# The gate products of a fused attention, expert and gate kernel as seven block products

## The chip, the cores and the metric

The kernel runs on one core of a Trainium2 chip. The metric is device time in microseconds (us) of one execution. TensorE (PE in the profile) multiplies, VectorE (DVE), ScalarE (ACT) and GpSimd (POOL) do the elementwise work, and SyncE (SP) issues the transfers.

## The reference

Three networks in a row. Attention with global and local keys gives `x` (1536 tokens x 512); a mixture of four experts turns it into a new `x` of the same shape; the last part, which the change touches, is:

```python
def _moe2_ref(x, w1, w2, w3, w_out):     # x 1536x512, w1 and w2 512x1024, w3 1024x1024, w_out 1024x512
    a = x @ w1
    b = x @ w2
    h = a * b @ w3
    return (h @ w_out).astype(np.float32)
```

The kernel takes the four weights of this part as float64 words and converts them to float32 on the chip while the experts run.

## The kernel before

Every product is made of blocks of 128x128 (stationary) by 128x512 (moving) and in three matmuls: an operand `x` is kept as two tiles of type fp32r, `hi` (its rounding) and `lo` (what the rounding left), and `three` (lines 52 to 56) adds hi*hi, hi*lo and lo*hi in one PSUM bank. `split` (lines 46 to 49) makes the two tiles: ACT casts, DVE (or POOL, if asked) subtracts.

The 1536 tokens are three chunks of 512. All engines run their instructions in the order in which the code issues them (`manual_schedule`), so that order is the schedule. After the attention and the experts, `experts_and_gate` does two things:

- the w34 stage (`for j in range(FC)`, 8 steps of 24 matmuls): w3 times w_out, once, with one split of the result per step and, behind it on ACT and DVE, the split (`land`) of the weight block that was loaded the step before. The weight block for step j + 4 is loaded in step j into the place `slots[4 + j % 4]` that step j used.
- the gate stage: for each chunk c and each of 8 blocks f of 128 hidden columns, `gate` makes a = x @ w1 and b = x @ w2 (2 x 12 matmuls of 512 columns), multiplies them, splits the product; `final`, one step later, adds its 12 matmuls into four PSUM banks. After the last f of a chunk four copies (`o`) and four transfers write its 512 rows of the output.

The PSUM pool `ps_z` has four banks for products, `ps_a` the four banks of `final`. `x_hi[c]`, `x_lo[c]` hold x split, `acc[c]` holds it whole. `slots` are eight pairs of tiles 128x1024 for split weights, and `wr` are two tiles for weights as they come from memory.

Of the kernel before, what the change touches and what calls it, by code (L numbers as in the profile page):

```python
# [8 lines left out]
F32 = mybir.dt.float32  # L9
F32R = mybir.dt.float32r  # L10
# [3 lines left out]
ALU = mybir.AluOpType  # L14
# [4 lines left out]
P = 128  # L19
# [506 lines left out]
def experts_and_gate(tc, g, x_hi, x_lo, slots, experts, first_time):  # L526

    nc = tc.nc
    name = "" if first_time else "g"
    with ExitStack() as ctx:  # L530
        big = ctx.enter_context(tc.tile_pool(name=name + "big", bufs=1))
        pool = ctx.enter_context(tc.tile_pool(name=name + "mp", bufs=2))
        ps_z = ctx.enter_context(tc.tile_pool(name=name + "ps_z", bufs=4, space=PSUM))
        ps_a = ctx.enter_context(tc.tile_pool(name=name + "ps_a", bufs=1, space=PSUM))
        acc = [big.tile([P, KC, CW], F32, name=f"acc{c}") for c in range(NCH)]
# [66 lines left out]
        for n, w in enumerate(work):  # L602
            if n >= done:
# [3 lines left out]
                elif coming:  # L607
                    s = coming[-1][0] + 1
# [12 lines left out]
            if n > 4 and n % FC not in (LAG - 1, LAG):  # L621
# [34 lines left out]
        pend = {}  # L656
        work2 = [(c, f) for c in range(NCH) for f in list(range(4, FC)) + list(range(4))]
        first, last = 4, 3

        def gate(c, f):  # L660
            hi, lo = slots[f]
            za = ps_z.tile([P, CW], F32, name="z")
            zb = ps_z.tile([P, CW], F32, name="z")
# [12 lines left out]
        def final(c, f):
            hh, hl = pend.pop((c, f))
            if f == first:
                g.acc_ps = [ps_a.tile([P, DM], F32, name=f"o{d}") for d in range(TPC)]
            for j in range(TPC):  # L680
                js = slice(j * P, (j + 1) * P)
                three(nc, g.acc_ps[j], hh[:, js], hl[:, js], w34h[:, f], w34l[:, f], f == first, f == last)
            if f == last:
                for j in range(TPC):
                    o = wpool.tile([P, DM], F32, name="o", bufs=4)
                    if j % 2:
                        nc.scalar.copy(o, g.acc_ps[j])
                    else:
                        nc.vector.tensor_copy(o, g.acc_ps[j])
                    t0 = c * CW + j * P  # L690
                    nc.sync.dma_start(g.out[t0 : t0 + P, :], o)
# [12 lines left out]
def tile_attention_experts_gate(
# [117 lines left out]
```

## Time and profile before

| | us |
|---|---|
| time, median of 3 runs | 854.98 (854.77 to 855.07) |
| the profiled execution's own time | 855.01 |
| its span, first to last instruction | 853.2 |
| PE busy in the span | 843.0 (99%), 4102 matmul records |
| DVE, ACT, POOL busy | 363.4 (43%), 242.2 (28%), 228.8 (27%) |
| mean granted clock | 0.998 |

The profile is of one execution. PE is the matmul engine and PEld its weight load. Matmuls are pipelined: a record's length is longer than the distance to the next one's start, and the ends are modelled, so the pace is read from starts. A timeline row reads: start, duration (both us), engine, line, operation, output <- inputs, shape, count, and in brackets the idle time before it and what ended it.

### The profile page before, as it was taken

What the parts mean: (1) busy time and instruction counts of PE and PEld (TensorE: products, weight loads), DVE (VectorE), ACT (ScalarE), POOL (GpSimd) and SP (SyncE); (2) the same over time, 40 slices, a digit from 0 to 9 for tenths busy, and PEclk for the clock granted to TensorE, in tenths of its full rate; (3) what the DMA queues carried; (4) which work ended last, traced back from release to release, by engine and by line L of the source; (5) the groups of instructions that cost most, each with busy time, mean ns of one, the idle gap of its engine ahead of it and who ended that gap; (6) DMA issues with size and microseconds to landing.
All of it is one profiled execution on the core that took longest, in us unless ns stands there. A gap on an engine that the chain in (4) does not pass through costs nothing.

```text
span 853.2 us, 10750 instructions
## 1 busy us (share of the span) xinstructions
PE 843.0 (99%) x4102; PEld 687.2 (81%) x4102; DVE 363.4 (43%) x745; ACT 242.2 (28%) x517; POOL 228.8 (27%) x246
## 2 busy tenths in 40 slices
PE   8999999999999999999999999999999999999996
PEld 4777888888888888888888888888888888888885
DVE  7998354547654547654223412123343412112111
ACT  6997221223221223221112201113233311111111
POOL 3687012514344445554120202121300000000000
PEclk9999999999999999999999999999999999999999
DMA  7761242548352537451203300002332201000001
GB/s 215 220 212 62 76 136 73 154 133 248 110 161 75 160 126 242 139 148 62 87 1 111 121 3 0 1 1 87 99 124 77 72 0 50 1 1 31 20 1 53
DMA packets 34287, 78.68 MB, mean 92 GB/s; under 512 B 3576, under 2 KB 10024, under 8 KB 34228
## 3 DMA queue, kind: packets, MB, share of 16 engines
q1 hardware_dynamic: 34228, 77.92, 29.2%
q8 instruction: 34, 0.56, 0.3%
q14 instruction: 25, 0.20, 0.1%
HBM read 64.25 MB, written 13.66 MB: 91 GB/s over the span
## 4 chain that ended last, share of the span: by engine, by line
PE 90%; POOL 3%; ACT 3%; DVE 1%; issue 1%; DMA 0%; SPq 0%; POOLq 0%; ACTq 0%; DVEq 0%
PE z L56 17%; PE z L55 17%; PE z L54 17%; PE o L56 13%; PE o L55 13%; PE o L54 13%; ACT pt L268 2%; POOL pt L307 2%; POOL sl L49 1%; ACT ptT L293 0%; DMA words<-in_n_local_dram 0%; PE sp L54 0%; DVE t L261 0%; PE sp L55 0%; PE sp L56 0%
## 5 line engine op out<-in xcount | busy, mean ns | idle before, releaser
L56 PE MATMUL z<-xh,sl 128*128 128x512 f32 x564 | 219.4, 389 | 0.0
L54 PE MATMUL z<-xh,sh 128*128 128x512 f32 x564 | 219.4, 389 | 0.0
L55 PE MATMUL z<-xl,sh 128*128 128x512 f32 x564 | 219.4, 389 | 0.0
L519 DVE SCALAR_TENSOR_TENSOR hl<-z,hh 128x512 fp32r<-128x512 f32 x93 | 64.2, 692 | 271.9 <-ACT hh L518 271.8
L518 ACT ACTIVATE hh<-z 128x512 fp32r<-128x512 f32 x93 | 55.4, 598 | 369.3 <-PE z L56 369.3
L54 PE MATMUL o<-hh,sh 128*128 128x512 f32 x384 | 149.5, 389 | 0.0
L55 PE MATMUL o<-hl,sh 128*128 128x512 f32 x384 | 149.4, 389 | 0.0
L56 PE MATMUL o<-hh,sl 128*128 128x512 f32 x384 | 149.4, 389 | 0.0
L56 PEld LDWEIGHTS z<-xh,sl 128*128 128x128 f32 x564 | 105.9, 188 | 22.3
L55 PEld LDWEIGHTS z<-xl,sh 128*128 128x128 f32 x564 | 105.9, 188 | 22.0
L54 PEld LDWEIGHTS z<-xh,sh 128*128 128x128 f32 x564 | 105.9, 188 | 21.8
L497 POOL TENSOR_TENSOR cr<-cr,cb 128x512 f32<-128x512 f32 x40 | 51.6, 1289 | 159.8 <-issue 153.5
L573 POOL TENSOR_TENSOR acc<-acc,t 128x512 f32<-128x512 f32 x36 | 47.6, 1343 | 161.3 <-DVE t L572 94.9
L54 PEld LDWEIGHTS o<-hh,sh 128*128 128x128 f32 x384 | 72.1, 188 | 15.1
L56 PEld LDWEIGHTS o<-hh,sl 128*128 128x128 f32 x384 | 72.1, 188 | 15.0
L55 PEld LDWEIGHTS o<-hl,sh 128*128 128x128 f32 x384 | 72.1, 188 | 14.8
L670 DVE TENSOR_TENSOR t<-z,t 128x512 f32<-128x512 f32 x24 | 16.6, 692 | 130.6 <-PE z L56 130.6
L49 DVE TENSOR_TENSOR sl<-wr,sh 128x1024 fp32r<-128x1024 f32 x49 | 60.4, 1235 | 26.1 <-ACT sh L48 26.0
L482 POOL TENSOR_SCALAR ca<-ca 128x512 f32<-128x512 f32 x40 | 59.6, 1489 | 37.0 <-DMA raw<-in_w_out_dram 37.0
L48 ACT CAST sh<-wr 128x1024 fp32r<-128x1024 f32 (+1 forms) x61 | 56.0, 920 | 5.4 <-DMA wr<-w3t_d 4.4
L268 ACT ACTIVATE pt<-t,negmax 128x256 f32<-128x256 f32 (+1 forms) x96 | 45.9, 479 | 9.0 <-DVE negmax L261 7.7
L307 POOL TENSOR_TENSOR pt<-pt,r 128x256 f32<-128x256 f32 (+1 forms) x72 | 40.8, 594 | 15.3 <-DVE r L236 12.6
(104 smaller groups left out, 846.8 us busy)
## 6 DMA issues: line engine op xcount, KB each, us to landing
wr<-in_w_moe_dram SPq DMA_DIRECT2D x32, 512.0 KB, 4.6
raw<-in_w3t_dram SPq DMA_DIRECT2D x16, 512.0 KB, 4.6
raw<-in_w_ab_dram SPq DMA_DIRECT2D x16, 512.0 KB, 4.2
raw<-in_w_out_dram SPq DMA_DIRECT2D x8, 512.0 KB, 5.7
w3t_d<-cr SPq DMA_DIRECT2D x16, 256.0 KB, 2.3
wab_d<-cr SPq DMA_DIRECT2D x16, 256.0 KB, 2.3
wr<-w3t_d SPq DMA_DIRECT2D x8, 512.0 KB, 3.4
wr<-wab_d SPq DMA_DIRECT2D x8, 512.0 KB, 3.2
```

Source lines behind the costliest of these rows:

```text
L48: nc.scalar.copy(hi, src)
L49: (lo_engine or nc.vector).tensor_tensor(lo, src, hi.bitcast(F32), op=ALU.subtract)
L54: nc.tensor.matmul(out, wh, xh, start=start, stop=False)
L55: nc.tensor.matmul(out, wh, xl, start=False, stop=False)
L56: nc.tensor.matmul(out, wl, xh, start=False, stop=stop)
L268: nc.scalar.activation(pt[:, hh, 0:w], t[:, 0:w], AF.Exp, bias=g.negmax[:, u * H + h : u * H + h + 1], scale=-1.0, accum_out=sums[:, h : h ...
L307: nc.gpsimd.tensor_tensor(pt[:, hh, 0:w], pt[:, hh, 0:w], r[:, hh : hh + 1].to_broadcast([P, w]), op=ALU.mult)
L482: nc.gpsimd.tensor_scalar(a, a, 2.0**-15, None, op0=ALU.max)
L497: nc.gpsimd.tensor_tensor(rest, rest, top.bitcast(F32), op=ALU.add)
L518: nc.scalar.activation(hh, z, AF.Relu)
L519: nc.vector.scalar_tensor_tensor(hl, z, 0.0, hh.bitcast(F32), op0=ALU.max, op1=ALU.subtract)
L573: nc.gpsimd.tensor_tensor(acc[c][:, d], acc[c][:, d], t, op=ALU.add)
```

## The change

For each f, the two products a and b of the gate form one block product: the rows are (w1 block, w2 block), the inner dimension is two halves of 256, and the columns are two groups of tokens. Done straight, it takes 8 products of blocks; the new class `Gate` does it in 7 by Strassen's scheme in Winograd's form, with sums of weight blocks (s1 to s4), sums of x blocks (t1 to t4), and sums of the products. In pair 0 the two groups are the halves of chunk 0 (256 tokens each), in pair 1 they are chunks 1 and 2 (512 each). The output of the last chunk is computed at the very end, from gated tiles that are kept aside in memory that has come free.

- In the w34 stage, weight blocks 4 to 7 of w3 go through two places (`slots[4]`, `slots[5]`) in place of four; block 6 is loaded in step 4 and split in step 5, block 7 in steps 5 and 6.
- Sums of x are made in DVE in steps 3 and 6, their splits in step 5; the first f's weights are prepared in steps 4 and 7.
- Weights are fetched and split for each f of each pair: 16 loads in place of 8, with the low parts made on POOL.
- The tile `o` for the output has 2 buffers in place of 4.

The core of the diff (index arithmetic of `Gate` left out):

```diff
-            hi, lo = slots[4 + j % 4]
+            hi, lo = slots[4 + (j if j < 4 else j % 2)]
...
             split(nc, w34h[:, j], w34l[:, j], z)
             land()
-            load_slot(4 + j % 4, g.w3t_f32[j + 4] if j < 4 else g.wab_f32[j])
+            if j in (0, 1, 4, 5):
+                load_slot(4 + j % 4 % 2, g.w3t_f32[{0: 4, 1: 5, 4: 6, 5: 7}[j]])
+            if j == 3:
+                gate.sums_of_x(0)
+                gate.fetch()
+            if j == 4:
+                gate.split_w(True)
+                gate.sums_of_w()
+            if j == 5:
+                for n in range(4):
+                    gate.split_x(0, n)
+            if j == 6:
+                gate.sums_of_x(1)
+            if j == 7:
+                gate.rest_of_acc()
+                gate.fetch()
+                gate.split_s(slots[4])
...
-            for z, o0 in ((za, 0), (zb, CW)):
-                for k in range(KC):
-                    ks = slice(o0 + k * P, o0 + (k + 1) * P)
-                    three(nc, z, hi[:, ks], lo[:, ks], x_hi[c][:, k], x_lo[c][:, k], k == 0, k == KC - 1)
...
+            o = wpool.tile([P, DM], F32, name="o", bufs=2)
...
+        for pair in range(2):
+            ps = [ps_a.tile([P, DM], F32, name=f"o{d}") for d in range(TPC)]
+            before = None
+            for f in range(FC + 1):
+                between = [()] * 4
+                if before:
+                    between = [(lambda j=j, h=before, f=f - 1: final(ps, h, f, (j,))) for j in range(TPC)]
+                if f < FC:
+                    before = gate.run(pair, f, between)
+                else:
+                    for j, issue in enumerate(between):
+                        issue()
+                        put(ps[j], pair, j)
+        for j in range(TPC):
+            z = {j: ps_z.tile([P, CW], F32, name="z")}
+            for f in range(FC):
+                final(z, gate.waiting[f], f, (j,))
+            put(z[j], NCH - 1, j)
...
+    def sums_of_w(self, part=None):
...
+        todo = ((s1, a21, a22, ALU.add), (s2, s1, a11, ALU.subtract), (s3, a11, a21, ALU.subtract),
+                (s4, a12, s2, ALU.subtract))
+        for out, a, b, op in todo if part is None else todo[part : part + 1]:
+            self.nc.vector.tensor_tensor(out, a, b, op=op)
+
+    def split_s(self, place=None):
+        y = place or self.places.pop(0)[1]
+        for c in (slice(0, 512), slice(512, F)):
+            split(self.nc, y[0][:, c], y[1][:, c], self.sums[:, c], self.nc.gpsimd)
...
+    def run(self, pair, f, between):
+        w = CW if pair else CW // 2
...
+        nc.scalar.copy(s1, product("a11", "b11"))
+        add(s6, s1, product("s2", "t2"))
+        if more:
+            self.split_w()
+        issue(0)
+        add(c11, s1, product("a12", "b21"))
+        part(0)
+        part(1)
+        add(u3, s6, product("s3", "t3"))
+        part(2)
+        part(3)
+        if more:
+            self.split_s()
+        issue(1)
+        z = product("s1", "t1")
+        add(c22, u3, z)
...
+        add(h2, s6, z)
+        issue(2)
+        z = product("a22", "t4")
...
+        add(h1, u3, z)
+        nc.vector.tensor_tensor(h1, h1, c11, op=ALU.mult)
+        split(nc, *halves[0], h1)
+        issue(3)
+        add(h2, h2, product("s4", "b22"))
+        nc.vector.tensor_tensor(h2, h2, c22, op=ALU.mult)
+        split(nc, *halves[1], h2)
+        if not pair and f in (2, 4):
+            self.split_x(1, 1 if f == 2 else 3)
+        if not pair and f == FC - 1:
+            self.split_x(1, 0)
+            self.split_x(1, 2)
+            self.make_waiting()
+        return hh, hl
```

`product` takes a bank `z` of `ps_z`, and issues `three` twice (the two parts of the inner half): 6 matmuls of w columns. `add` is a DVE addition of 128 x w; `issue(n)` issues the three matmuls of `final` for output rows n of the f before; `part(n)` makes one sum of the next f's weights; `split_w` splits the next f's plain weight blocks (768 columns).

On ACT, the end of the w34 stage stood like this before (`w34h<-z` splits the result of steps 5, 6 and 7, `sh4` to `sh6` are places of split weights, of which those written here are first read in the gate stage):

```order
L48 CAST w34h_5264<-z_5419 128x512 [waits PE_49]
L48 CAST sh4_1556<-wr_5417 128x1024 [waits DMAHW4_49,DVE_49]
L48 CAST w34h_5264<-z_5450 128x512 [waits PE_49]
L48 CAST sh5_1558<-wr_5448 128x1024 [waits DMAHW5_49,DVE_49]
L48 CAST w34h_5264<-z_5481 128x512 [waits PE_49]
```

and stands like this now (`z_5430`, `z_5469`, `z_5502` are the results of steps 5, 6 and 7; step 6 reads `sh4`, step 7 reads `sh5`):

```order
L48 CAST w34h_5264<-z_5430 128x512 [waits PE_49]
L48 CAST sh4_1556<-wr_5415 128x1024 [waits DMAHW3_49,DVE_49]
L48 CAST sh6_1560<-acc0_1576 128x512 [waits DVE_49] x2
L48 CAST sl6_1561<-acc0_1576 128x512 [waits DVE_49]
L48 CAST sl6_1561<-acc0_1576 128x512
L48 CAST w34h_5264<-z_5469 128x512 [waits PE_49]
L48 CAST sh5_1558<-wr_5459 128x1024 [waits DMAHW4_49,Activation_49]
L48 CAST w34h_5264<-z_5502 128x512 [waits PE_49]
L48 CAST sh4_1556<-sums_5425 128x512 [waits DVE_49]
L48 CAST sh4_1556<-sums_5425 128x512
```

The cast of a weight place stands behind the result of the step that comes right ahead of the step that reads it; the sums of the first f's weights stand behind the result of step 7.

On PE, the w34 stage passed to the gate stage like this before (the last matmul of step 7, then the first product of `gate`):

```order
L56 MATMUL z_5481<-sh3_83,sl7_1563 128x512
L54 MATMUL z_5514<-xh0_71,sh4_1556 128x512 [waits Activation_49]
L55 MATMUL z_5514<-xl0_74,sh4_1556 128x512 [waits Pool_49]
L56 MATMUL z_5514<-xh0_71,sl4_1557 128x512 [waits DVE_49]
L54 MATMUL z_5514<-xh0_71,sh4_1556 128x512
```

and does like this now (the last matmul of step 7, the product a11 b11, and the first three matmuls of s2 t2, whose stationary operands `sh4`, `sl4` hold the sums):

```order
L56 MATMUL z_5502<-sh3_83,sl5_1559 128x512
L54 MATMUL z_5543<-xh0_71,hh_5417 128x256
L55 MATMUL z_5543<-xl0_74,hh_5417 128x256 [waits Pool_49]
L56 MATMUL z_5543<-xh0_71,hl_5418 128x256 [waits Pool_49]
L54 MATMUL z_5543<-xh0_71,hh_5417 128x256
L55 MATMUL z_5543<-xl0_74,hh_5417 128x256
L56 MATMUL z_5543<-xh0_71,hl_5418 128x256
L54 MATMUL z_5551<-sl6_1561,sh4_1556 128x256 [waits Activation_49]
L55 MATMUL z_5551<-sl7_1563,sh4_1556 128x256
L56 MATMUL z_5551<-sl6_1561,sl4_1557 128x256 [waits Pool_49]
```

The matmuls now have 256 columns, and the second product waits for ACT's and POOL's split of sums.

On ACT, the passage from chunk 0 to the next one was this before (`o` is an output copy, `z_5939` the first product of chunk 1):

```order
L48 CAST hh_5911<-t_5908 128x512 [waits DVE_49]
L687 COPY o_5930<-o1_5587 128x512 [waits PE_49]
L687 COPY o_5936<-o3_5589 128x512 [waits PE_49]
L669 COPY t_5965<-z_5939 128x512 [waits PE_49,Activation_49]
L48 CAST hh_5968<-t_5965 128x512 [waits DVE_49]
```

and is this now, from pair 0 to pair 1 (`sh0`, `sh1` take the last two split sums of x, `prob_6328` is s1 of pair 1's first f):

```order
L48 CAST hh_6273<-t_6261 128x256 [waits DVE_49]
L48 CAST sh0_77<-acc1_1577 128x1024 [waits PE_49,Pool_49]
L48 CAST sh1_79<-acc1_1577 128x1024 [waits PE_49,Pool_49]
L683 COPY o_6309<-o1_5539 128x512 [waits PE_49]
L683 COPY o_6321<-o3_5541 128x512 [waits DMAHW0_49,PE_49,Activation_49]
L835 COPY prob_6328<-z_6329 128x512 [waits PE_49]
```

The second output copy now waits for a transfer (DMAHW0, the output of the first copy), and the copy that frees the first product's bank stands behind it.

## Rows read from the trace of the kernel before

**Rows 1.** The page: busy time, and the chain that ended last

```profile
PE 843.0 (99%) x4102; PEld 687.2 (81%) x4102; DVE 363.4 (43%) x745; ACT 242.2 (28%) x517; POOL 228.8 (27%) x246
PE 90%; POOL 3%; ACT 3%; DVE 1%; issue 1%; DMA 0%; SPq 0%; POOLq 0%; ACTq 0%; DVEq 0%
```

**Rows 2.** Timeline: first matmul of the w34 stage, last matmul of the kernel

```profile
606.92 0.39 PE L54 MATMUL z<-sh,sh 128*128 128x512 f32 x1
...
846.06 0.39 PE L56 MATMUL o<-w34h,hl 128*128 128x512 f32 x1
```

**Rows 3.** Timeline of weight loads, one burst of the attention scores

```profile
29.64 0.30 PEld L250 LDWEIGHTS sp<-keys,qr 64*128 64x128 f32 x4 [0.17 <-issue]
```

**Rows 4.** Tile sp: durations (ns, least/median/most) of loads and matmuls

```profile
L250 PEld LDWEIGHTS sp<-keys,qr x18: 182/186/187, 29.6 to 36.0; 64*128 64x128 f32 x18
L250 PE MATMUL sp<-keys,qr x18: 376/376/480, 29.6 to 36.0; 64*128 64x256 f32 x18
```

**Rows 5.** Timeline around the end of one step of the w34 stage

```profile
639.34 0.39 PE L56 MATMUL z<-sh,sl 128*128 128x512 f32 x1
639.34 0.19 PEld L54 LDWEIGHTS z<-sh,sh 128*128 128x128 f32 x1
639.56 0.39 PE L54 MATMUL z<-sh,sh 128*128 128x512 f32 x1
639.76 0.59 ACT L48 CAST w34h<-z 128x512 fp32r<-128x512 f32 x1 [3.90 <-PE z L56]
...
640.25 1.06 ACT L48 CAST sh<-wr 128x1024 fp32r<-128x1024 f32 x1
640.38 0.69 DVE L49 TENSOR_TENSOR w34l<-z,w34h 128x512 fp32r<-128x512 f32 x1 [3.27 <-ACT w34h L48]
641.34 1.23 DVE L49 TENSOR_TENSOR sl<-wr,sh 128x1024 fp32r<-128x1024 f32 x1 [0.26 <-ACT sh L48]
```

**Rows 6.** Groups by shape: busy us, mean ns, idle before

```profile
L400 DVE TENSOR_TENSOR xl<-op,xh 128x256 fp32r<-128x256 f32 x24 | 9.9, 413 | 0.6 <-ACT xh L394 0.4
L49 DVE TENSOR_TENSOR hl<-t,hh 128x512 fp32r<-128x512 f32 x24 | 16.6, 693 | 16.5 <-ACT hh L48 16.5
L311 DVE TENSOR_SCALAR pt<-pt,r 128x256 f32<-128x256 f32 x20 | 12.4, 618 | 0.1
L394 ACT CAST xh<-op 128x256 fp32r<-128x256 f32 x24 | 8.8, 367 | 0.6 <-PE op L326 0.6
L48 ACT CAST hh<-t 128x512 fp32r<-128x512 f32 x24 | 14.9, 621 | 69.2 <-DVE t L670 69.2
L48 ACT CAST sh<-wr 128x256 fp32r<-128x256 f32 x12 | 4.9, 405 | 0.0
L576 POOL TENSOR_TENSOR xl<-acc,xh 128x512 fp32r<-128x512 f32 x12 | 15.5, 1290 | 8.8 <-ACT xh L575 8.8
L49 POOL TENSOR_TENSOR sl<-wr,sh 128x256 fp32r<-128x256 f32 x12 | 8.7, 728 | 0.6 <-ACT sh L48 0.3
```

**Rows 7.** The page, DMA issues: KB each, median us to landing

```profile
wr<-wab_d SPq DMA_DIRECT2D x8, 512.0 KB, 3.2
out_dram<-o SPq DMA_DIRECT2D x12, 256.0 KB, 2.6
```

**Rows 8.** Tile out_dram: the twelve output transfers

```profile
DMA to landing us min/median/max: 2.1/2.6/4.6
```

**Rows 9.** Timeline: the last output copy

```profile
846.48 0.59 ACT L687 COPY o<-o 128x512 f32<-128x512 f32 x1 [0.77 <-PE o L56]
```

**Rows 10.** Windows: busy us by engine (instructions), granted clock, DMA share, GB/s

```profile
16.00:100.00 84.00, 82.83 (x735) 62.89 (x734) 67.78 (x254) 66.71 (x226) 50.45 (x96) 1.00 0.47 146
848.00:849.00 1.00, 0.00 (x0) 0.00 (x0) 0.00 (x0) 0.00 (x0) 0.00 (x0) 1.00 1.10 385
850.00:851.00 1.00, 0.00 (x0) 0.00 (x0) 0.00 (x0) 0.00 (x0) 0.00 (x0) 0.50 0.08 16
```

More of the change, by code (lines that the diff above doesn't have):

```diff
@@ L676, in final @@
[L676 to L691, printed above, removed]
@@ new lines, in experts_and_gate, with final @@
+            if j == 5:
[7 more added lines that the diff above has]
+                gate.split_s(slots[4])
+        def final(ps, hid, f, js, f0=0, f1=FC - 1):
+            hh, hl = hid
+            for j in js:
+                ts = slice(j * P, (j + 1) * P)
+                three(nc, ps[j], hh[:, ts], hl[:, ts], w34h[:, f], w34l[:, f], f == f0, f == f1)
@@ new lines, in put @@
+        def put(ps, c, j):
+            o = wpool.tile([P, DM], F32, name="o", bufs=2)
+            if j % 2:
+                nc.scalar.copy(o, ps)
+            else:
+                nc.vector.tensor_copy(o, ps)
+            t0 = c * CW + j * P
+            nc.sync.dma_start(g.out[t0 : t0 + P, :], o)
+        for pair in range(2):
[7 more added lines that the diff above has]
+                    before = gate.run(pair, f, between)
+                else:
+                    for j, issue in enumerate(between):
+                        issue()
+                        put(ps[j], pair, j)
@@ new lines, in experts_and_gate, with __init__, rest_of_acc, make_waiting @@
+        for j in range(TPC):
[3 more added lines that the diff above has]
+            put(z[j], NCH - 1, j)
+class Gate:
+    def __init__(self, tc, g, big, pool, ps_z, wpool, hidden, x_hi, x_lo, acc, slots):
+        self.nc, self.g, self.big, self.pool, self.ps_z, self.wpool = tc.nc, g, big, pool, ps_z, wpool
+        self.hidden = hidden
+        self.x_hi, self.x_lo, self.acc, self.slots = x_hi, x_lo, acc, slots
+        self.order = [(pair, f) for pair in range(2) for f in range(FC)]
+        self.fetched, self.sums, self.made = [], None, []
+        halves = lambda t: [t[i][:, h * CW : (h + 1) * CW] for i in range(2) for h in range(2)]
+        self.parts = [
+            list(zip(halves(slots[6]), halves(slots[7]))), [slots[0], slots[2], slots[1], slots[3]],
+        ]
+        self.places = [(slots[0], slots[1]), (slots[4], slots[5])] * 4 + [(slots[6], slots[7]), (slots[4], slots[5])] * 4
+    def rest_of_acc(self):
+        t = self.big.tile([P, KC, CW], F32, name="acc0")
+        self.tmp = [t[:, i] for i in range(KC)]
+    def make_waiting(self):
+        self.waiting = [(self.x_hi[0][:, i], self.x_lo[0][:, i]) for i in range(KC)]
+        h, l = (self.big.tile([P, KC, CW], F32R, name=f"acc{i}") for i in (1, 2))
+        self.waiting += [(h[:, i], l[:, i]) for i in range(KC)]
+    def block(self, of, pair, k, n):
+        ks = slice(2 * k, 2 * k + 2)
+        if pair:
+            return of[1 + n][:, ks]
+        return of[0][:, ks, n * (CW // 2) : (n + 1) * (CW // 2)]
+    def sums_of_x(self, pair):
+        sub = lambda out, a, b: self.nc.vector.tensor_tensor(out, a, b, op=ALU.subtract)
+        b11, b12, b21, b22 = (self.block(self.acc, pair, k, n) for k in range(2) for n in range(2))
+        sub(b11, b12, b11)
+        sub(b12, b22, b12)
+        sub(b22, b22, b11)
+        sub(b21, b21, b22)
+    def parts_of(self, pair, n):
+        return [t.rearrange("p (k t) -> p k t", k=2) for t in self.parts[pair][n]]
+    def split_x(self, pair, n):
+        split(self.nc, *self.parts_of(pair, n), self.block(self.acc, pair, n // 2, n % 2))
+    def x_operand(self, pair, what):
+        if what[0] == "b":
+            k, n = int(what[1]) - 1, int(what[2]) - 1
+            return self.block(self.x_hi, pair, k, n), self.block(self.x_lo, pair, k, n)
+        return self.parts_of(pair, "1342".index(what[1]))
+    def fetch(self):
+        if self.order:
+            pair, f = self.order.pop(0)
+            raw = self.pool.tile([P, F], F32, name="wr")
+            self.nc.sync.dma_start(raw, self.g.wab_f32[f])
+            self.fetched.append(raw)
+    def split_w(self, first=False):
+        raw = self.fetched[0]
+        if first:
+            a, b = ([self.hidden.tile([P, CW], F32R, name=n) for n in ("hh", "hl")] for _ in range(2))
+        else:
+            a, b = [t[:, 0:512] for t in self.places[0][0]], [t[:, 512:768] for t in self.places[0][0]]
+        b = [t[:, 0:256] for t in b]
+        split(self.nc, *a, raw[:, 0:512], self.nc.gpsimd)
+        split(self.nc, *b, raw[:, 768:], self.nc.gpsimd)
+        part = lambda of, i: [t[:, i * 256 : (i + 1) * 256] for t in of]
+        self.blocks = dict(a11=part(a, 0), a12=part(a, 1), a22=b)
+    def sums_of_w(self, part=None):
+        if part in (None, 0):
+            self.sums = self.wpool.tile([P, F], F32, name="sums")
+        raw = self.fetched[0]
+        a11, a12, a21, a22 = (raw[:, i * 256 : (i + 1) * 256] for i in range(4))
+        s1, s2, s3, s4 = (self.sums[:, i * 256 : (i + 1) * 256] for i in range(4))
+        todo = ((s1, a21, a22, ALU.add), (s2, s1, a11, ALU.subtract), (s3, a11, a21, ALU.subtract),
[6 more added lines that the diff above has]
+            split(self.nc, y[0][:, c], y[1][:, c], self.sums[:, c], self.nc.gpsimd)
+        for i in range(4):
+            self.blocks[f"s{i + 1}"] = [t[:, i * 256 : (i + 1) * 256] for t in y]
+        self.made.append(self.blocks)
+        self.fetched.pop(0)
+        self.fetch()
+    def run(self, pair, f, between):
+        nc = self.nc
+        w = CW if pair else CW // 2
+        blocks = self.made.pop(0)
+        def product(a, b):
+            z = self.ps_z.tile([P, CW], F32, name="z")[:, 0:w]
+            h, l = blocks[a]
+            xh, xl = self.x_operand(pair, b)
+            for k in range(2):
+                ks = slice(k * P, (k + 1) * P)
+                three(nc, z, h[:, ks], l[:, ks], xh[:, k], xl[:, k], k == 0, k == 1)
+            return z
+        def issue(n):
+            if between[n]:
+                between[n]()
+        more = bool(self.fetched)
+        add = lambda out, a, b: nc.vector.tensor_tensor(out, a, b, op=ALU.add)
+        part = (lambda n: self.sums_of_w(n)) if more else (lambda n: None)
+        s1 = self.pool.tile([P, CW], F32, name="prob")[:, 0:w]
+        s6, u3, c22, c11 = (t[:, 0:w] for t in self.tmp)
+        nc.scalar.copy(s1, product("a11", "b11"))
[14 more added lines that the diff above has]
+        add(c22, u3, z)
+        h2 = self.pool.tile([P, CW], F32, name="t", bufs=3)[:, 0:w]
+        add(h2, s6, z)
+        issue(2)
+        z = product("a22", "t4")
+        if pair:
+            hh = self.hidden.tile([P, CW], F32R, name="hh")
+            hl = self.hidden.tile([P, CW], F32R, name="hl")
+            halves = [(hh, hl), self.waiting[f]]
+        else:
+            hh = self.hidden.tile([P, CW], F32R, name="hh")
+            hl = self.hidden.tile([P, CW], F32R, name="hl")
+            halves = [(hh[:, 0:w], hl[:, 0:w]), (hh[:, w:], hl[:, w:])]
+        h1 = self.pool.tile([P, CW], F32, name="t", bufs=3)[:, 0:w]
+        add(h1, u3, z)
[12 more added lines that the diff above has]
+        return hh, hl
```

23 lines of the change are left out of this document (1 added, 22 removed).

## The prediction

> **What bounds the kernel now.** I read the page's busy times and chain first [rows 1]: PE is busy for 99% of the span and 90% of the chain is PE. The question is then whether PE waits or runs at its pace, and the starts answer that: from the first matmul of the w34 stage to the last of the kernel there are 8 x 24 + 864 = 1056 matmuls, started from 606.92 to 846.06 [rows 2], so 239.14 / 1055 = 0.2267 us each, which is also the distance of two neighbours (639.34 and 639.56 [rows 5]). There is no gap: this stretch is matmul count times 0.2267, and a stall anywhere in it adds in full. What follows the last matmul is a copy that starts 0.42 later and takes 0.59 [rows 9], and an output transfer.
>
> **What is removed.** The gate stage has 3 chunks x 8 f x (24 + 12) = 864 matmuls of 512 columns, 195.9 us. After the change pair 1 has 8 x 7 x 6 = 336 matmuls of 512 columns (384 before for the same two chunks), `final` keeps its 288: 624 x 0.2267 = 141.5 us. Pair 0 has 8 x 7 x 6 = 336 matmuls of 256 columns where 192 of 512 were. So the change saves 54.4 us less 336 times p, the pace at 256 columns, which no row shows for this type.
>
> **The pace p.** 0.2267 at 512 columns is 512 / 2.4 GHz = 0.213 plus 0.013. If the 0.013 belongs to each matmul, p is 0.107 + 0.013 = 0.120. It can't be below what the load of 128 weight columns takes. A load's record is 0.19 long and begins with its predecessor's matmul [rows 5], yet records overlap: the four loads of one burst [rows 3], two for each half of the array, end 0.30 after the first one's start, so the second on a half starts 0.30 - 0.19 = 0.11 after the first. And a matmul of the scores that has to wait for its load is 480 ns long in place of 376 [rows 4]: the load holds it for 0.104. Lower end 0.110. Upper end, if a load isn't hidden under a matmul this short: 0.104 + half of 0.2267 = 0.217. I take 0.120, since at 512 columns the load hides fully and at 256 it still fits (0.11 in 0.12): 336 x 0.120 = 40.3, total 181.8, saving 14.1 us.
>
> The Trainium skill (TensorE: Matmul & The Clock Gate, "Back-to-back issue gap") gives columns / 2.4 + 2.5 ns, 109 ns at 256 columns; by it the sum would be 3.7 us lower, but at 512 it says 216 where the rows have 227, so it is 11 ns low here.
>
> **What it adds on PE's path.** Five stalls, each from durations of [rows 5, 6] (I count 0.42 from a bank's last matmul start to the reader's start [rows 5], or 0.2 from its end).
>
> (a) Steps 6 and 7 of the w34 stage. The weight block of step 6 is split right behind step 5's result, and that of step 7 behind step 6's, so the splits start when the reader is due. The chain is in [rows 5], where it costs nothing as its result is read later: last matmul start 639.34, ACT's cast of the result 639.76, cast of the weights 640.25, DVE's low part 641.34 to 642.57. A step's third matmul needs the low part; it is due at 639.34 + 3 x 0.227 = 640.02. Stall 2.6 us with the wake-up, twice: 5.2.
>
> (b) The start of the gate. After the last matmul start of step 7: cast of the result to 0.91, cast of s1, s2 to 1.53, POOL's low part 1.29, so 2.85. The second product's third matmul is due at 0.227 + 8 x 0.120 = 1.19. Stall 1.7. Its second half on POOL ends at 4.15, when the fourth product wants it: nothing.
>
> (c) Inside pair 0. A step on PE is 42 x 0.120 + 12 x 0.2267 = 7.8 us, but the first has no `final` in it: 5.0. DVE has 15 operations of 256 columns a step (11 on products, 4 sums of weights): 15 x 0.413 = 6.2, and waits twice for an ACT cast (0.42): 7.0. POOL has 3 x 1.29 + 0.73 = 4.6, ACT 3.4 (0.37 + 0.62 + 0.41 + 2 x 0.62 + 2 x 0.37). So DVE is covered except in the first step. There the second step's weight sums are ready at 6.8 after (b)'s origin (four products, then six DVE operations), cast 7.4, low part 8.8; due 7.9. Stall 0.9. Two splits of x for pair 1 (DVE 1.23 each, behind f 2 and f 4) put DVE back again; I count 0.3. Together 1.2. Weight loads (3.2 us [rows 7]) have a step of 7.8: covered.
>
> (d) From pair 0 to pair 1. `final` of the last f waits for low parts, 0.2 + 0.3. The larger wait comes from the two `o` buffers. From the end of pair 0's last product: DVE ends h2 at 2.35 and two low parts of 1024 columns at 5.5, copies row block 0 until 6.2; SP issues that transfer, then that of block 1, which ACT copied long before but which is queued behind. With 2.6 us to landing [rows 7] it lands at 9.25. ACT's copy of block 3 waits for that, and the copy of the first product of pair 1 is queued behind: it ends at 10.4. On PE `final` ends at 3.2, four products (5.44) fill the four banks by 8.65, and the fifth waits for that copy: 1.8. DVE, late by as much, delays the next `final` by 0.65. Together 2.9.
>
> (e) At the end of pair 1 `final` follows the last product directly; the low part of h1 takes 0.2 + 4 operations of 0.62 to 0.69 = 2.9, due at 2.5: 0.5. Inside pair 1 a step is 54 x 0.2267 = 12.2 on PE and 11 x 0.693 + 4 x 0.413 + 2 x 0.66 = 10.6 on DVE: covered.
>
> Sum of stalls: 5.2 + 1.7 + 1.2 + 2.9 + 0.5 = 11.5.
>
> **What it gives at the end.** Before, four transfers of 256 KB follow within 2 us and the last lands after 4.6; now the last one stands alone 5.4 us behind its predecessor. The least is 2.1 [rows 8], and SP is free when it comes: 2.2 us less (bounds 1.5 and 2.7).
>
> **The sum** against the profiled execution's 855.0 (the median is 854.98, so no correction): 855.0 - 14.1 + 11.5 - 2.2 = 850.2.
>
> **Rivals.**
>
> 1. Loads show at 256 columns (slower). Place: pair 0. p = 0.217 gives 336 x 0.097 = 32.6 more, 882.8. It decides from p = 0.120 + 4.8 / 336 = 0.134 on, where the time is back at 855. For it: in all rows of 128-column loads of this kind the load's record ended before the next matmul began (0.19 of 0.227 [rows 5]), so nothing closer has been seen in a steady run. Against it: two loads 0.11 apart, and a matmul held for 0.104 only [rows 3, 4]. The Trainium skill (TensorE: Matmul & The Clock Gate, "The mechanism") says that a weight load overlaps running matmuls only when it is for another group of rows; by that rule each matmul here would pay load and stream, which is this rival. The trace disagrees with it at 512 columns: 0.104 and 0.213 make 0.317, and the pace is 0.2267. Chance 0.12, everything above p = 0.134 included.
>
> 2. DVE becomes the bound in pair 0 (slower). A 256-column operation took 618 ns at line 311, with POOL at work beside it [rows 6]. Then a step is 15 x 0.618 + 0.84 = 10.1, eight make 81 against 59.4 + 1.2: 20 us more, 870. Against: L311 is a scalar operation; the two-tensor form with POOL beside it took 413 (L400). Chance 0.07.
>
> 3. The chains run later than worked out, by some 0.3 us in each of the 16 steps, since ACT, DVE and POOL wait in order on each other: about 5 more, 855, no change. For it: (c) leaves DVE only 0.8 of 7.8 us. Chance 0.13.
>
> 4. The stalls of (a) don't appear, because splits are done before they are due: 5.2 less, 845.0. Against it is the order on ACT. Chance 0.08.
>
> A fall of the clock in the stalls I leave out of the sum: between 16 and 100 us PE was idle in pieces and the granted clock stayed 1.00 (2.4 GHz); it stayed so from 848 to 849 too, with no matmul since 846.4, and was 0.50 from 850 to 851 [rows 10]. The gaps of (a) are shorter, 1.9 and 1.0.
>
> **How the numbers follow.** My forecast has a chance of 0.60; its own range is 846.8 (p = 0.110) to 853. With rival 4 below and rival 3 above, 844.5 to 860 holds 0.81; rivals 1 and 2 are left out above. A difference of 0.2% (1.7 us) is about what a measurement of this kernel tells from none. Faster by more: 0.57 of my forecast, 0.08 of rival 4, 0.03 of rival 3: 0.68. Within: 0.03 and 0.06: 0.09. Slower: 0.04 of rival 3, and rivals 1 and 2: 0.23.
>
> **What would show it.** Starts of the matmuls of 256 columns 0.120 apart where nothing waits (rival 1: 0.13 to 0.22). Two holes of 2.6 us on PE in steps 6 and 7 of the w34 stage, ended by ACT and then DVE, and one of 1.7 at the second product, ended by POOL. DVE busy about 6.2 of 7.8 us in pair 0. One hole near 1.8 at the fifth product of pair 1, ended by ACT behind a transfer. The last transfer landing about 2.2 us after its issue. I am wrong if the 256-column starts are further apart than 0.134, or if holes of PE behind the w34 stage sum to more than 16 us.

## The result, and the profile after

The changed kernel takes 863.16 us (median of 5 runs, 862.86 to 864.24) against 854.98 (5 runs, 854.34 to 855.07): a ratio of 1.0101, 95% interval 1.0086 to 1.0116. It is slower by 8.2 us where 4.8 us faster was predicted, and lies outside the predicted range. The profiled execution took 862.86, its span is 861.1.

The page of the changed kernel, busy time and the chain that ended last, against [rows 1]:

```profile
PE 840.1 (98%) x4198; PEld 683.6 (79%) x4198; DVE 476.1 (55%) x945; ACT 266.8 (31%) x581; POOL 307.1 (36%) x310
PE 79%; DVE 9%; issue 4%; ACT 4%; POOL 3%; DMA 0%; SPq 0%; POOLq 0%; ACTq 0%; DVEq 0%
```

PE's share of the chain fell from 90% to 79% and DVE's rose from 1% to 9%: the path now runs through DVE. The timeline of the first matmul of the w34 stage and of the last of the kernel, with the last output copy behind it, against [rows 2, 9]:

```profile
606.92 0.39 PE L54 MATMUL z<-sh,sh 128*128 128x512 f32 x1
...
855.14 0.39 PE L56 MATMUL z<-w34h,acc 128*128 128x512 f32 x1
...
855.61 0.59 ACT L683 COPY o<-z 128x512 f32<-128x512 f32 x1 [10.29 <-PE z L56]
```

The stretch between the two matmuls was 239.1 us and is 248.2. I split it as the prediction did, from the start of each matmul to the start of the next: 512 columns take 0.2267 where nothing waits, and 256 columns 0.119. What is over that is stall.

| term | predicted | measured |
|---|---|---|
| saving by fewer and shorter matmuls | -14.1 | -14.4 |
| (a) steps 6 and 7 of w34 | 5.2 | 5.3 |
| clock at 1.2 GHz behind them | 0 | 1.7 |
| (b) start of the gate | 1.7 | 1.9 |
| (c) inside pair 0 | 1.2 | 7.9 |
| (d) pair 0 to pair 1 | 2.9 | 5.5 |
| (e) end of pair 1 | 0.5 | 0.7 |
| delays too small to be placed | 0 | 0.5 |
| behind the last matmul | -2.2 | -1.2 |
| sum | -4.8 | 7.9 |

855.0 + 7.9 = 862.9, and the execution took 862.9. A second stretch at the low clock lies inside (d) and is counted there (1.6 of its 5.5). Next in the timeline, against [rows 5], are the holes of (a) and (b) and the pace at 256 columns:

```profile
641.35 0.50 PE L54 MATMUL z<-sh,sh 128*128 128x512 f32 x1 [1.62 <-ACT sh L48]
641.68 0.40 PE L55 MATMUL z<-sl,sh 128*128 128x512 f32 x1
642.60 0.50 PE L56 MATMUL z<-sh,sl 128*128 128x512 f32 x1 [0.52 <-DVE sl L49]
...
658.81 2.52 POOL L49 TENSOR_TENSOR sl<-sums,sh 128x512 fp32r<-128x512 f32 x2 [21.14 <-ACT sh L48]
660.14 0.39 PE L56 MATMUL z<-sl,sl 128*128 128x256 f32 x1 [0.85 <-POOL sl L49]
...
676.46 0.28 PE L54 MATMUL z<-xh,sh 128*128 128x256 f32 x1
676.58 0.28 PE L55 MATMUL z<-xl,sh 128*128 128x256 f32 x1
```

The reader sees the hole of step 6 ended by ACT and then by DVE, that of the second product ended by POOL, and 0.12 between two matmuls of 256 columns: as predicted, in place and in size. The hole of step 7 has the same two parts.

The windows of the changed kernel around the w34 stage's end and the passage of the pairs (span, busy us of PE, PEld, DVE, ACT, POOL with counts, granted clock, DMA share, GB/s), against [rows 10]:

```profile
651.00:654.40 3.40, 3.40 (x9) 2.65 (x9) 3.19 (x3) 0.00 (x0) 0.00 (x0) 0.50 0.49 154
654.40:729.60 75.20, 69.34 (x438) 59.34 (x438) 61.41 (x124) 28.34 (x60) 42.94 (x34) 1.00 0.18 57
729.60:733.00 3.40, 3.40 (x10) 2.61 (x9) 2.41 (x4) 2.78 (x4) 0.00 (x0) 0.51 0.00 0
```

Twice the clock stood at 0.50, which is 1.2 GHz, for 3.4 us: behind the hole of step 7, and after the holes at the end of pair 0. In the kernel before, the granted clock is 1.00 from the first matmul of the w34 stage to the last of the kernel (606.92 to 846.28).

Now to (c), the large one. DVE's groups by shape in the gate stage, against [rows 6]:

```profile
L799 DVE TENSOR_TENSOR sums<-wr 128x256 f32<-128x256 f32 x30 | 21.7, 723 | 0.0
L799 DVE TENSOR_TENSOR sums<-wr,sums 128x256 f32<-128x256 f32 x15 | 13.8, 923 | 0.0
L799 DVE TENSOR_TENSOR sums<-sums,wr 128x256 f32<-128x256 f32 x15 | 12.2, 816 | 0.5
L49 DVE TENSOR_TENSOR hl<-t,hh 128x256 fp32r<-128x256 f32 x16 | 11.0, 690 | 7.6 <-ACT hh L48 7.6
L831 DVE TENSOR_TENSOR acc<-acc,z 128x256 f32<-128x256 f32 x16 | 6.5, 407 | 0.0
```

All five have 128x256 elements and one kind of work. The last, which reads a product from PSUM (`z`), takes 407 ns, as the 413 of line 400 in [rows 6] said. The four that read SBUF only take 690 to 923. Those of line 799 are means over both pairs; in pair 0 alone (655 to 731) they are, in ns, least/median/most:

```profile
L799 DVE TENSOR_TENSOR sums<-wr x16: 410/632/1404, 662.0 to 725.5; 128x256 f32<-128x256 f32 x16
L799 DVE TENSOR_TENSOR sums<-sums,wr x8: 843/844/845, 662.9 to 724.4; 128x256 f32<-128x256 f32 x8
L799 DVE TENSOR_TENSOR sums<-wr,sums x8: 408/412/413, 664.3 to 725.8; 128x256 f32<-128x256 f32 x8
```

`sums<-wr` are the first and the third sum of a step, `sums<-sums,wr` is the second, `sums<-wr,sums` the fourth: in pair 0 the first two take long and the last two don't. The timeline of one step, some rows of POOL and DVE, tells when:

```profile
672.92 2.87 POOL L49 TENSOR_TENSOR sl<-sums,sh 128x512 fp32r<-128x512 f32 x2 [1.01 <-ACT sh L48]
675.12 0.96 DVE L49 TENSOR_TENSOR hl<-t,hh 128x256 fp32r<-128x256 f32 x1 [0.47 <-ACT hh L48]
677.34 0.42 DVE L49 TENSOR_TENSOR hl<-t,hh 128x256 fp32r<-128x256 f32 x1 [0.47 <-ACT hh L48]
678.17 2.17 POOL L49 TENSOR_TENSOR sl<-wr,sh 128x512 fp32r<-128x512 f32 x2 [2.38 <-ACT sh L48]
678.34 1.40 DVE L799 TENSOR_TENSOR sums<-wr 128x256 f32<-128x256 f32 x1
679.78 0.84 DVE L799 TENSOR_TENSOR sums<-sums,wr 128x256 f32<-128x256 f32 x1
680.55 0.41 DVE L831 TENSOR_TENSOR acc<-acc,z 128x256 f32<-128x256 f32 x1
680.88 0.41 DVE L799 TENSOR_TENSOR sums<-wr 128x256 f32<-128x256 f32 x1
```

The low part `hl` took 0.96 at 675.12, while POOL worked until 675.79, and 0.42 at 677.34, when POOL was idle; the sum that began at 678.34, 0.17 after a low part on POOL, took 1.40, and a sum of the same form at 680.88, after POOL had ended at 680.34, took 0.41. And PE waits for it; PE's timeline at the same step's start:

```profile
675.14 0.50 PE L54 MATMUL o<-w34h,hh 128*128 128x512 f32 x1
675.48 0.39 PE L55 MATMUL o<-w34l,hh 128*128 128x512 f32 x1
676.13 0.50 PE L56 MATMUL o<-w34h,hl 128*128 128x512 f32 x1 [0.26 <-DVE hl L49]
```

The third matmul waits for `hl`, whose 0.96 in place of 0.42 is seen in the rows before. None of PE's waits between 666 and 728 ends on POOL: they end on DVE (`hl`) and on ACT, whose casts wait for DVE in their turn. So POOL delays PE there through DVE, and not by being late itself. The seven steps from one such place to the next (666.70 to 728.15) take 61.45 / 7 = 8.8 us each; 7.8 was predicted.

### The profile page after: what moved, and what is told of

Its sections match the earlier page's. It is cut to its first block, busy times and chain, and to the rows that moved or that the text cites. A ratio compares the mean times of both kernels' runs of the same rounds, so it can differ in the third digit from the quotient of the medians.

```text
span 861.1 us, 11406 instructions
## 1 busy us (share of the span) xinstructions
PE 840.1 (98%) x4198; PEld 683.6 (79%) x4198; DVE 476.1 (55%) x945; ACT 266.8 (31%) x581; POOL 307.1 (36%) x310
## 4 chain that ended last, share of the span: by engine, by line
PE 79%; DVE 9%; issue 4%; ACT 4%; POOL 3%; DMA 0%; SPq 0%; POOLq 0%; ACTq 0%; DVEq 0%
PE z L56 15%; PE z L54 15%; PE z L55 14%; PE o L56 11%; PE o L54 11%; PE o L55 11%; DVE sums L799 3%; ACT pt L268 2%; POOL pt L307 2%; DVE acc L831 1%; DVE t L831 1%; POOL sl L49 1%; DVE hl L49 1%; ACT hh L48 1%; DVE t L865 1%
## 5 line engine op out<-in xcount | busy, mean ns | idle before, releaser
L54 PE MATMUL z<-xh,sh 128*128 128x512 f32 (+1 forms) x464 | 176.0, 379 | 0.0
L56 PE MATMUL z<-xh,sl 128*128 128x512 f32 (+1 forms) x464 | 175.8, 379 | 0.0
L55 PE MATMUL z<-xl,sh 128*128 128x512 f32 (+1 forms) x464 | 175.8, 379 | 0.0
L55 PEld LDWEIGHTS z<-xl,sh 128*128 128x128 f32 x464 | 87.2, 188 | 17.0
L56 PEld LDWEIGHTS z<-xh,sl 128*128 128x128 f32 x464 | 87.2, 188 | 16.9
L54 PEld LDWEIGHTS z<-xh,sh 128*128 128x128 f32 x464 | 87.2, 188 | 16.7
L54 PE MATMUL z<-sh,sh 128*128 128x512 f32 (+1 forms) x160 | 60.0, 375 | 3.9 <-ACT sh L48 3.2
L48 ACT CAST sh<-wr 128x256 fp32r<-128x256 f32 (+1 forms) x83 | 61.6, 761 | 5.4 <-PE o L56 2.6
L49 POOL TENSOR_TENSOR sl<-wr,sh 128x256 fp32r<-128x256 f32 (+1 forms) x42 | 41.6, 1005 | 59.0 <-ACT sh L48 53.8
L56 PE MATMUL z<-sh,sl 128*128 128x512 f32 (+1 forms) x160 | 59.6, 373 | 1.0 <-DVE sl L49 1.0
```

## The experiments

In each, the stretch named is from the first matmul of the w34 stage to the last matmul of the kernel (248.2 in the changed kernel), read from starts in the trace. The theory: the failure is DVE's SBUF-only operations held up beside POOL's low parts; the w34 holes and their clock are a separate cost. The rivals: that DVE simply has too much work in pair 0 whoever makes the low parts, and that the loss is mostly the holes and the clock.

**1. Split early.** The next weight block is split ahead of the step's result.

```diff
+            land()
             split(nc, w34h[:, j], w34l[:, j], z)
-            land()
```

> The split of the weight block that came in is issued ahead of the split of the step's result in the w34 stage. Theory (the w34 holes are the late split alone, and the fall of the clock behind them is a consequence): both holes of 2.7 us go, and the 3.4 us at 1.2 GHz at 651 us with them (1.7): 863.2 - 7.1 = 856.1. Rival (the clock falls at the start of the gate products for another reason): only the holes go, 857.8, and 0.50 is still granted near 651.

Measured 856.07 against 854.79, ratio 1.0017 (1.0008 to 1.0027). The stretch is 241.3, 7.0 less, which is the 5.3 of (a) and the 1.7 of the clock. The windows over the stage's end and over the passage from pair 0 to pair 1:

```profile
639.00:655.00 16.00, 14.67 (x75) 12.25 (x74) 11.87 (x16) 6.93 (x13) 3.23 (x3) 1.00 0.31 99
715.00:745.00 30.00, 26.45 (x120) 20.14 (x120) 23.71 (x38) 11.05 (x21) 11.25 (x10) 1.00 0.20 70
```

The clock stays at 1.00 in both. The cost of (a) is the order of issue alone. Here the second fall of the clock is gone as well, and yet the passage has 5.4 us of stalls, as many as in the changed kernel (5.5): that fall cost nothing by itself.

**2. Holes filled.** Eleven matmuls whose results are overwritten go ahead of steps 6 and 7, so that PE works while it would wait.

```diff
+            if j in (6, 7):
+                for _ in range(11):
+                    nc.tensor.matmul(z, slots[0][0][:, 0:P], slots[1][0][:, 0:CW], start=True, stop=True)
```

> Eleven more matmuls of 512 columns in front of steps 6 and 7 of the w34 stage, into the bank that the step then starts anew; their operands are there, so they run while the split is waited for. Theory (idle PE in the holes makes the clock fall): the third matmul of a step starts when it did, the stretch from 651 to 654 runs at 2.4 GHz, 1.7 us less: 861.5. Rival (the clock falls for the wait at the gate's start, or anything else): 863 and 0.50 granted near 651 as now.

Measured 862.99 in one execution: the time is the rival's, but the clock near 651 is not. Its windows tell why (the start of the kernel, and the end of w34):

```profile
13.60:17.00 3.40, 3.22 (x18) 2.13 (x20) 2.40 (x15) 3.31 (x14) 1.74 (x5) 0.54 0.74 200
651.00:655.00 4.00, 4.00 (x18) 3.03 (x17) 3.64 (x4) 0.12 (x1) 0.00 (x0) 1.00 0.37 125
```

In this execution the clock was low at 13.6 to 17.0, far ahead of the edit, and its w34 stage began at 608.54 in place of 606.92. The stretch after that is 246.8, 1.4 less. With PE busy through the hole the clock stays up behind it: the idle time brought the fall, not the work that follows. The size is shown by one execution only. At the passage, where the second fall is gone too, the stalls are 5.5 again.

**3. Narrow low parts on POOL.** POOL's low parts in the gate stage are cut to 32 of their columns.

```diff
+    def split_narrow(self, hi, lo, src):
+        self.nc.scalar.copy(hi, src)
+        n = slice(0, 32)
+        self.nc.gpsimd.tensor_tensor(lo[:, n], src[:, n], hi[:, n].bitcast(F32), op=ALU.subtract)
...
-            split(self.nc, y[0][:, c], y[1][:, c], self.sums[:, c], self.nc.gpsimd)
+            self.split_narrow(y[0][:, c], y[1][:, c], self.sums[:, c])
```

> POOL makes only 32 columns of each low part of the gate's weights (the rest of the low tiles keeps what was in them, so that part of the result is left out). Theory (DVE's additions on SBUF alone are slowed by POOL's subtractions that run beside them, and that makes the chain late in pair 0): the sums of weights take 0.41 to 0.45 us in place of 0.72 to 0.92, the low parts of 256 columns 0.43 in place of 0.69, a step of pair 0 takes 7.8 us in place of 8.8, the excess of pair 0 falls from 7.9 to about 1: 863.2 - 7 = 856, or 854.5 if the second fall of the clock goes too. Rival (DVE is slow because transfers and ACT use the same weight tiles): durations and step stay, 863.

Measured 849.99 against 854.79, ratio 0.9938 (0.9921 to 0.9955), some 6 us below what was expected, which had counted little but (c). DVE's groups in this kernel (the sums are line 808 here):

```profile
L808 DVE TENSOR_TENSOR sums<-wr 128x256 f32<-128x256 f32 x30 | 12.6, 419 | 0.0
L49 DVE TENSOR_TENSOR hl<-t,hh 128x256 fp32r<-128x256 f32 x16 | 6.8, 425 | 7.6 <-ACT hh L48 7.6
```

DVE's instructions are the same as in the changed kernel; only what POOL does beside them is shorter. The sums fell from 723 to 419 ns. The stretch is 235.6, 12.6 less, and it falls in three places: (c) 7.9 to 0.2, the passage (d) 5.5 to 1.6, (b) 1.9 to 0.7 (that one since PE waits for POOL's shorter low part itself). One step of pair 0, between two starts of the same matmul:

```profile
688.13 0.40 PE L54 MATMUL o<-w34h,hh 128*128 128x512 f32 x1
...
695.91 0.40 PE L54 MATMUL o<-w34h,hh 128*128 128x512 f32 x1
```

7.78: the 7.8 that the prediction had for PE.

**4. Low parts on DVE.** POOL makes none of them in the gate stage; DVE has their work on top of its own.

```diff
-        split(self.nc, *a, raw[:, 0:512], self.nc.gpsimd)
-        split(self.nc, *b, raw[:, 768:], self.nc.gpsimd)
+        split(self.nc, *a, raw[:, 0:512])
+        split(self.nc, *b, raw[:, 768:])
...
-            split(self.nc, y[0][:, c], y[1][:, c], self.sums[:, c], self.nc.gpsimd)
+            split(self.nc, y[0][:, c], y[1][:, c], self.sums[:, c])
```

> DVE makes the low parts of the gate's weights in place of POOL. Theory (POOL beside it slows DVE): the sums of weights take 0.41 to 0.45 us, the low parts of 256 columns 0.43; DVE's work in a step of pair 0 is 15 x 0.42 + 3 x 0.69 + 0.42 + 0.84 = 9.6 us in place of 8.8 now, so 6 us more: 869. Rival (durations do not hang on POOL): the sums stay at 0.72 to 0.92, a step takes 11 or more, 880 and above.

Measured 867.84 (one execution). DVE's groups:

```profile
L799 DVE TENSOR_TENSOR sums<-wr 128x256 f32<-128x256 f32 x30 | 12.6, 419 | 0.0
L49 DVE TENSOR_TENSOR hl<-t,hh 128x256 fp32r<-128x256 f32 x16 | 6.8, 425 | 7.5 <-ACT hh L48 7.5
L49 DVE TENSOR_TENSOR sl<-sums,sh 128x512 fp32r<-128x512 f32 x32 | 21.9, 688 | 1.9
```

With POOL silent each operation is at its short time, though DVE has more of them. So it isn't the load on DVE that makes them long, and the rival on DVE's amount of work falls as an account of the durations. It is right about something else: the low parts don't fit on DVE either, and the kernel is slower for it.

**5. More places for output copies.** On top of experiment 1, the third and fourth output copy of pair 0's chunk use tiles that stand idle then, so that no copy waits for a transfer.

```diff
-            o = wpool.tile([P, DM], F32, name="o", bufs=2)
+            if c == 0 and j == 2:
+                o = pool.tile([P, DM], F32, name="t", bufs=3)
+            elif c == 0 and j == 3:
+                o = pool.tile([P, DM], F32, name="prob")
+            else:
+                o = wpool.tile([P, DM], F32, name="o", bufs=2)
```

> The kernel with the early split (856.07), and the third and fourth output copies of chunk 0 go to two other tiles, so that no copy waits for a transfer there. Theory (the hole at the fifth product of pair 1 is the second copy's wait for a transfer on ACT, which holds the copy of the first product): the holes of 1.0 at 730 and 2.0 at 737 to 740 go but for some 0.7, and ACT's and DVE's waits for out_dram (4.4 and 2.2) go: 2.3 less, 853.8. Rival (DVE is late there anyway, by the last splits of x and its own backlog): the hole stays at 1 to 2 us with DVE as its end, 855 to 856.

Measured 853.73 against 854.73, ratio 0.9991 (0.9982 to 1.0001), 2.3 less than experiment 1; the stretch is 238.1, 3.1 less. The waits of the changed kernel from 600 on that this takes away at the passage (total, times, longest):

```profile
ACT o L683 <- DMA out_dram<-o: 4.4, 1, 4.4
```

The passage keeps 2.4 us of stalls at its first part, where `final` waits for the last f. So the two buffers `o` are worth 3.1 here. The hole that the prediction named, at the fifth product of pair 1, is not in the changed kernel's trace, where PE comes there late through its own low clock. In experiment 1, without that fall, it is there, 1.0 us, and ACT ends it:

```profile
731.15 0.50 PE L54 MATMUL z<-sh,sh 128*128 128x512 f32 x1 [0.73 <-ACT prob L835]
```

**6. Chunk 0 straight.** The w34 stage as before the change, chunk 0 by 8 products as before, and only chunks 1 and 2 by 7.

```diff
+            hi, lo = slots[4 + j % 4]
...
+        for f in range(FC):
+            hid = straight(f)
+            land()
...
+            if before:
+                final(ps, before, f - 1, range(TPC))
...
+                now = gate.run(1, f, between)
```

> Only chunks 1 and 2 as seven block products; chunk 0 straight as before (24 matmuls of 512 columns a step), with the w34 stage as before. Theory (the pair of 512 columns pays, the pair of halves loses more on DVE than it saves on PE): the matmuls take 239.1 - 48 x 0.2267 = 228.3, stalls 0.7 at the end of pair 1 and up to 1 at the passage, no clock fall, 1.2 less behind the last matmul: 855.0 - 10.9 + 1.2 - 1.2 = 844. Rival (pair 1 itself is covered only because pair 0 and its weights were prepared ahead; with DVE near 10 of 12.2 us a step it falls late): 848 to 852.

Measured 850.94 against 854.73, ratio 0.9963 (0.9949 to 0.9977), 7 us above what was expected. The time is in the rival's range (848 to 852), but most of the loss is not where the rival put it, in pair 1. The waits between 655 and 716 name it:

```profile
PEld z L56 <- DVE sl L49: 5.8, 6, 1.0
```

Six steps of chunk 0 wait for the low part of their weights, with 0.80 of lost pace each (4.8); 2.3 more are lost where pair 1 begins and 0.7 at its end. I had put `land()` behind the products: the same late split as (a), made again by my own order.

**7. The same with the order mended.** The split stands ahead of the products, pair 1's first weights are prepared one step earlier, and the first 21 matmuls of chunk 2's output stand between pair 1's last product and its last `final`.

```diff
-            hid = straight(f)
             land()
+            if f == FC - 1:
+                gate.split_w()
+                gate.sums_of_w()
+                gate.split_s()
+            hid = straight(f)
...
+        for f in range(FC - 1):
+            final(z, gate.waiting[f], f, (0,))
+        for j, issue in enumerate(between):
+            issue()
+            put(ps1[j], 1, j)
+        final(z, gate.waiting[FC - 1], FC - 1, (0,))
```

> The kernel with chunk 0 straight (850.94), with its weight split ahead of the step that runs beside it, the first weights of pair 1 prepared one step earlier, and the first 21 matmuls of the last chunk ahead of the last final of chunk 1. Theory (what is left over in that kernel are only these late chains: 6 x 0.80 in the straight steps, 2.3 at the passage, 0.7 at the end of pair 1): 7.8 less, 843.2, and PE without a hole from the w34 stage to the end. Rival (the holes move to the next chain): 846 to 850.

Measured 842.82 (842.64 to 843.23) against 854.32, ratio 0.9862 (0.9846 to 0.9879): 11.5 us faster than the kernel before, 20 faster than the changed one. Its page, and the window over w34 and gate:

```profile
PE 831.4 (99%) x4054; PEld 677.8 (81%) x4054; DVE 430.6 (51%) x841; ACT 256.9 (31%) x545; POOL 265.5 (32%) x278
```

```profile
606.00:840.00 234.00, 229.44 (x1013) 189.71 (x1011) 129.19 (x176) 66.68 (x108) 46.93 (x40) 1.00 0.18 60
```

The stretch is 228.25 for 1008 matmuls: 1007 x 0.2267 = 228.3. No stall is left in it. The 48 matmuls that pair 1 saves are worth 10.9 us when nothing waits; low parts still run on POOL, but a step of pair 1 has 12.2 us on PE and covers what DVE loses (one sum of each step still takes 1.5 us there).

**8. POOL writes only.** On top of experiment 3, each low part on POOL is two memsets in place of a subtraction: POOL is busy, and reads nothing.

```diff
-        self.nc.gpsimd.tensor_tensor(lo[:, n], src[:, n], hi[:, n].bitcast(F32), op=ALU.subtract)
+        for _ in range(2):
+            self.nc.gpsimd.memset(lo.bitcast(F32), 0.0)
```

> POOL fills each low part of the gate's weights with zeros, twice, in place of the subtraction (the low parts are left out of the result): POOL stays busy for a like time, but reads nothing. Theory (DVE's operations on two operands in SBUF wait for POOL instructions that read SBUF): the sums take 0.41 to 0.45 us and the low parts of 256 columns 0.43, as with POOL nearly idle, a step of pair 0 7.8 us, 850 to 851. Rival (any work of POOL slows DVE, or POOL's results are late): sums at 0.7 and more, a step 8.5 or more, 857 to 863.

Measured 850.02 (one execution). POOL's and DVE's groups (the sums are line 809 here):

```profile
L798 POOL MEMSET sl<- 128x512 f32 x86 | 44.8, 526 | 46.3 <-PE z L56 43.7 <-PE z L55 0.2
L809 DVE TENSOR_TENSOR sums<-wr 128x256 f32<-128x256 f32 x30 | 12.6, 419 | 0.0
L49 DVE TENSOR_TENSOR hl<-t,hh 128x256 fp32r<-128x256 f32 x16 | 6.8, 425 | 7.7 <-ACT hh L48 7.7
```

In the first 65 us of the gate stage POOL works about three quarters as much as in the changed kernel (29.4 us from 655 to 720 against 37.6), and DVE's operations are at 419 and 425. The two engines do work at the same time; two rows of one step of pair 0:

```profile
677.79 2.78 POOL L798 MEMSET sl<- 128x256 f32 x6 [2.42 <-PE z L56]
679.17 0.43 DVE L49 TENSOR_TENSOR hl<-t,hh 128x256 fp32r<-128x256 f32 x1 [0.53 <-ACT hh L48]
```

In pair 0 the trace has 35 DVE operations of 256 columns with both inputs in SBUF that ran beside a memset, 9 of them sums, and none took more than 0.43. So it is not that POOL is busy, but that it reads SBUF while DVE takes two inputs from there.

## Why the prediction was wrong

The step that failed is (c), "Inside pair 0", in its line "15 x 0.413 = 6.2". The 0.413 was that of line 400, an operation with one input in PSUM. Eight of the fifteen in a step (four sums, two multiplications, two low parts) have both inputs in SBUF, and POOL's subtractions read SBUF beside some of them. Three of the eight are held in every step of pair 0: the first sum (0.85 to 1.40), the second (0.84) and the first low part (0.95 to 0.96). That is 1.4 to 1.9 us more than three operations of 0.42, where the prediction had left DVE 0.8 of 7.8. DVE then has no slack, and PE's stalls are 7.9 in place of 1.2. Of this 1.6 falls in the first step, where I had 0.9; four steps lose 0.65 each at the wait for `hl`; and the two steps in which DVE splits x for pair 1 lose 1.86 each, where I had 0.3 for both. Experiment 3 shows the cause by taking it away (7.9 to 0.2), 4 and 8 that neither DVE's load nor POOL's being busy is enough.

I had the sign before me and dismissed it. Rival 2 took 618 ns from line 311, an operation that ran beside POOL, and I set it aside as being of another kind, with line 400 as proof that the two-tensor form isn't slowed. The proof had the wrong operands. What I should have asked is whether any row showed an operation with both inputs in SBUF with POOL at work. In the gate stage none could; the window of before over it:

```profile
657.00:846.00 189.00, 189.00 (x835) 156.56 (x834) 41.85 (x58) 35.90 (x57) 0.00 (x0) 1.00 0.06 20
```

POOL has no instruction there (the fifth pair, x0), so every DVE duration of [rows 6] from that stage was taken without it. But the same trace has the case earlier, in the w34 stage:

```profile
620.02 1.30 POOL L576 TENSOR_TENSOR xl<-acc,xh 128x512 fp32r<-128x512 f32 x1 [0.73 <-ACT xh L575]
620.93 1.47 DVE L49 TENSOR_TENSOR sl<-wr,sh 128x1024 fp32r<-128x1024 f32 x1 [10.70 <-ACT sh L48]
```

The same DVE operation takes 1.23 in [rows 5]; here it began while POOL subtracted, and took 1.47. Rival 2's place was right and its price too large (20 us): only some of the operations meet a low part on POOL, and PE's 7.8 us a step cover much. Rival 3 had the delay nearly in size for pair 0 (5) but put it down to engines that wait for each other in order, and to both pairs; pair 1 lost 0.7.

The Trainium skill (SBUF — State Buffer, "Who interferes with whom") states just this: a VectorE instruction with two inputs in SBUF contends with a GpSimd instruction that reads SBUF, and not with one that only writes; the one that comes second waits until the first has ended. The trace agrees in all three: 419 ns alone, 1.40 us for a sum that started 0.17 after POOL's, 419 beside memsets. I read the page for the change and didn't hold this rule against the eight operations.

The other terms. **The pace** was right (0.119 for 0.120) and rival 1 with it wrong: weight loads are hidden at 256 columns. **(a)**, **(b)** and **(e)** were right in place, order of releasers and size; rival 4 did not happen. **The clock**, which I left out since the gaps of (a) were shorter than others that did no harm, fell behind the second of them: 1.7. The fall behind pair 0 cost nothing, since the passage waits for other things anyway (5.4 without it in experiment 1). **(d)** was mis-sized: 5.5 for 2.9. The chain through the two `o` buffers is there and is worth 3.1 beside POOL's low parts (experiment 5 against 1). With POOL's low parts short and the same two buffers, (d) falls by 3.9, to 1.6 (experiment 3). The two make more than 5.5 together, so they overlap. **The end** gave 1.2 for 2.2: the last transfer, alone as predicted, took 3.1 to land, where I had taken the least of [rows 8], 2.1; why it took longer stays open.

Added up, 12.6 of the 23.5 us of stalls belong to POOL's low parts by experiment 3, and 7.0 to the order in the w34 stage by experiment 1; the two don't overlap in place. What stays open is why the first hole of (a), as large as the second, brought no fall of the clock.

## What to carry to other kernels

Before a duration is carried from one place to another, ask where each input lies and which engine worked beside it: an addition or subtraction of 128x256 took 0.41 us with an input in PSUM, 0.42 with both in SBUF, and in pair 0 up to 1.40 with both in SBUF while POOL read. And a scheme that trades matmuls for elementwise work pays only where the step on PE is long enough to cover that work: here the pair of chunks with 12.2 us a step gave the full 10.9 us (48 matmuls), while the halves with 7.8 saved 192 x 0.2267 - 336 x 0.119 = 3.5 and lost 7.9. Split an operand ahead of the result that is due at the same time, or the split starts when its reader should.

## What the runs showed of the hardware

- A matmul of 512 columns that is woken by a wait is followed by the next one 0.335 later, not 0.227 (675.14 to 675.48 above): each wait costs 0.108 on top of its length. The prediction's "with the wake-up" held it for (a), and didn't count it for the many small waits of (c).
- The granted clock was 0.50 for 3.4 us behind a hole of 2.7 us on PE (in two parts, with two matmuls between them), stayed at 1.00 behind one of the same size 8 us earlier, and fell in neither place when matmuls filled them.
- A DVE operation that met POOL's subtraction was not slowed in proportion but held until POOL was done. All 24 held operations of pair 0 (three in each of eight steps, 256 columns) ended 0.28 after the end of a subtraction on POOL, however long that left them: the 1.40 of 678.34 and the 0.84 of 679.78 ended at 679.75 and 680.62, POOL's two at 679.47 and 680.34. In pair 1 the held multiplications of 512 columns ended 0.55 after POOL.
- The engine that comes second is the one that waits, and that can be POOL: its low part of 256 columns took 0.92 beside DVE, 0.73 in [rows 6], and those of 512 columns up to 1.55, against 1.29. So not every operation that overlaps with POOL is held: the fourth sum of each step of pair 0 began ahead of a subtraction and the first multiplication as one ended, and both stayed at 0.41 to 0.43.
